# Top-k attention and GELU MLP on one core: the last 64 rows' P turned by VectorE squares and DRAM instead of by TensorE

## The chip, the cores and the metric

The kernel runs on one core of a Trainium2 chip. The metric is the device time of one launch in microseconds; three runs of the kernel before gave 1480.06 us in the median (1479.93 to 1480.07). PE is TensorE (PEld its weight loads), DVE VectorE, ACT ScalarE, POOL GpSimd, SP the engine whose queue issues most DMAs.

## The reference

Eight batches, eight heads, 576 rows, head size 64. Per head, only the 32 largest scores of a row take part in the softmax; the attention's output, as 4608 tokens of width 512, goes through an MLP with an exact GELU. All is float32.

```python
scores = scale * np.matmul(q, k.transpose(0, 1, 3, 2))
kth = np.partition(scores, -32, axis=-1)[..., -32:-31]
scores = np.where(scores >= kth, scores, -1e9)
attn = np.exp(scores - max); attn = attn / (sum + 1e-9)
x = (attn @ v) as (B*S, H*D)          # 4608 x 512
out = gelu_exact(x @ w_in) @ w_out    # 512 -> 2048 -> 512
```

## The kernel before

**Items and slots.** Two heads make a pair, four pairs (`NP`) a batch. A pair's 576 query rows are four tiles of 128 (`t` = 0 to 3, `NM` = 4) and 64 last rows (`TL`). An item is one tile of one pair: 128 rows for two heads, 2 x 576 scores in one tile `s`. The last 64 rows of two pairs share one item (`t == NM`), so a batch has 16 main items and 2 of last rows, 144 items in all (`N`). Even batches put the two items of last rows at their end, odd batches at their start (`starts` holds each batch's first item). So four items of last rows stand together four times: 16 to 19, 52 to 55, 88 to 91 and 124 to 127. Below, such a group from 52 on is called a boundary; there are three.

**The slot.** One loop (`for n in range(ahead)`) writes out the order of every engine by hand; pass n is slot n. In slot n: scores of items n+2 and n+3 (in even slots), into PSUM and from there by ACT into `s` (L394); the products with v of item n-3 (`attend`, L715 and L726); the transposes of item n-2 (`transposes`: `tails` L619/L622 and `both` L649, copied by ACT into `pt`, L664); `select` and `softmax` of item n-1 on ACT (L517, L529); `top_k` of item n on DVE (MAX8 and MATCH_REPLACE8, L483 and L486), which ends with `inverse` (L504, the reciprocal of item n-1's sums) and has `square_p` in its middle; on POOL `threshold` (L497, L498), `normalise` (L552), two passes over the scores for the lists (L447, L455), `add_small` (L510); and MLP pieces (`mlp`): `h_ps` (L773), then `gelus` on ACT (L789, with a table load), sums of the gelus on POOL (L810 to L813), `seven_piece` (L927) and the `y_ps` products (L929), whose parts POOL adds up (L950, L979 to L994).

**Two ways to turn P.** The products need P with the keys on the partitions. For most items PE transposes it: one matmul of `tails` (two for an item of last rows) and eight of `both`, and ACT copies them from PSUM. For an item that `squared(i)` names (even main items from 28 on), DVE transposes `s` in squares of 32 x 32 in place (L569), four DMAs of SP write it to a DRAM tile `turned` (L579) at the end of slot i+2, and four read it back (L586) into `pt` at the start of slot i+3. `pt` has one buffer for two items, so a read waits until the products of the items before are done; last rows use the left half of `pt` and a tile of their own, `pt_end`, item by item.

**What is shared.** From slot 13 on (`few`), one PSUM bank `z` serves the last keys' scores, the tails' transposes, the `seven` product and the attention output `o` in turn: each waits until ACT has copied the one before it out. The first of two score tiles in an even slot shares its banks with `h_ps`. `issue` holds a v load back to the end of the slot (`flush`) where a square's DMAs come first (`held`). `room_in` says how many MLP pieces a slot gets.

```python
    def squared(i):
        return SINGLE.stop - 2 < i < N - 2 and i % 2 == 0 and items[i][1] < NM and i % RINGS != 12
```

Of the kernel before, what the change touches and what calls it, by code (L numbers as in the profile page):

```python
# [8 lines left out]
TOPK = 32  # L9
# [5 lines left out]
def kernel(  # L15
# [95 lines left out]
    def load(n, pair, queue=None, queue2=None):  # L111
        if pair >= n_pairs:
            return
        queue = queue or nc.sync
        queue2 = queue2 or queue
        b, h0 = pair // NP, 2 * (pair % NP)
        src = sources[n]
        if n != "v" and pair >= SQUARES:
            t = flat[n][0]
            for e in range(2):  # L120
                for d in range(2):
# [8 lines left out]
        for e in range(2):  # L130
            queue.dma_start(
                out=t[:, 0:NM, e, :], in_=src[b, h0 + e, 0:SM].rearrange("(t p) d -> p t d", p=P)
            )
            queue2.dma_start(out=t[e * TL : (e + 1) * TL, NM, e, :], in_=src[b, h0 + e, SM:S])
# [35 lines left out]
    low = const.tile([P, 1], f32, name="low")  # L170
    nc.gpsimd.memset(low, -EXP0 * 2.0**20)
    high = const.tile([P, 1], f32, name="high")
# [103 lines left out]
    def transpose_qk(pair, first=False):  # L276
# [4 lines left out]
        def squares(c):  # L281
            rq, rk, kt = flat["q"][0], flat["k"][0], kt_of.get(pair)
            if c == 0:
                nc.vector.transpose(kt[:, 0:q_tail], rk)
            elif c == 1:
                nc.vector.transpose(kt[:, q_tail:], rq[:, SM:])
            else:
                nc.vector.transpose(q_of[pair], rq[:, 0:SM])

        def by_pe(c):  # L290
            rq, rk = raw_of("q", pair), raw_of("k", pair)
            group = (
                [(rk, j) for j in range(NM)], [(rk, NM), (rq, NM)], [(rq, j) for j in range(NM)]
            )[c]
            tp = bank("tp_qk")
            for x, (r, j) in enumerate(group):
                nc.tensor.transpose(
                    tp[:, x * P : (x + 1) * P], r[:, j].rearrange("p e d -> p (e d)"), ident
                )
            dst = (kt_of[pair][:, 0:SM], kt_of[pair][:, SM:], q_of.get(pair))[c]  # L300
            copy = nc.vector.tensor_copy if first and c < 2 else nc.scalar.copy
            copy(out=dst, in_=tp[:, 0 : len(group) * P])

        def piece(c):
            if c == 0:
                kt_of[pair] = work.tile([P, 2 * P + SM], f32, tag="kt", bufs=NP + 2, name="kt")
# [17 lines left out]

    def row(i, e):
        return S_of[i][:, e * S : (e + 1) * S]
# [10 lines left out]
    def halves(t, e, step):  # L337

        return spread(t[:, e * TL :], step + (TL if e == 0 else -TL), TL)

# [3 lines left out]
    def last_keys(i, t_ps):  # L344
# [3 lines left out]
        if t < NM:  # L348
            nc.tensor.matmul(
                t_ps[:, 0:P], lhsT=q_of[pair][:, t * P : (t + 1) * P],  # L350
                rhs=kt_of[pair][:, SM : SM + P], start=True, stop=True,
# [8 lines left out]
        for r in range(2):  # L360
            kt = kt_of[pair + r]
            for e in range(2):
                nc.tensor.matmul(
                    t_ps[half(r, e), r * TL : (r + 1) * TL],
                    lhsT=kt[:, SM + P + e * TL : SM + P + (e + 1) * TL],
                    rhs=kt[:, SM + e * TL : SM + (e + 1) * TL],
# [3 lines left out]
            s.rearrange("p (r n) -> p r n", r=2)[:, :, SM:S],  # L370
            t_ps[:, 0:P].rearrange("p (r n) -> p r n", r=2), func=AF.Copy, scale=scale,
        )

    def scores(i, second=False):
# [3 lines left out]
        S_of[i] = s = work.tile([P, 2 * S], f32, tag="s", bufs=6, name="s")  # L378
# [3 lines left out]
        if t < NM:  # L382
            q_t, kt = q_of[pair][:, t * P : (t + 1) * P], kt_of[pair]
            for e in range(2):
                rows = slice(e * D, (e + 1) * D)
                nc.tensor.matmul(  # L386
                    s_ps[:, e], lhsT=q_t[rows, :], rhs=kt[rows, 0:SM], start=True, stop=True
# [7 lines left out]
        else:  # L395

            for r in range(2):
                kt = kt_of[pair + r]
                for e in range(2):
                    rows = slice(e * D, (e + 1) * D)  # L400
                    nc.tensor.matmul(
                        s_ps[half(r, e), r, :], lhsT=kt[rows, SM + P + e * TL : SM + P + (e + 1) * TL],
                        rhs=kt[rows, 0:SM], start=True, stop=True,
                    )
            s2 = s.rearrange("p (r n) -> p r n", r=2)
            nc.scalar.activation(s2[:, :, 0:SM], s_ps, func=AF.Copy, scale=scale)
# [50 lines left out]
    def top_k(i, last, middle):  # L457
# [4 lines left out]
            "neg": work.tile([P, 2], f32, tag="neg", name="neg"),  # L462
            "bias": work.tile([P, 2], f32, tag="bias", name="bias"),
            "den": work.tile([P, 2], f32, tag="den", name="den"),
            "rden": work.tile([P, 2], f32, tag="rden", name="rden"),
        }
        top = work.tile([P, 2, TOPK - 8], f32, tag="top", bufs=1, name="top")
        into = [st["first"]] + [top[:, :, 8 * r : 8 * r + 8] for r in range(TOPK // 8 - 1)]
# [21 lines left out]
        st["kth"] = top[:, :, TOPK - 9]  # L490
# [45 lines left out]
    def normalise(i):  # L536
# [4 lines left out]
        if i < DIAGS:  # L541
            d = work.tile([P, 2, P], f32, tag="part", bufs=3, name="diag")
# [12 lines left out]
    pt_end = const.tile([P, 2, P], f32, name="pt_end")  # L555
    nc.gpsimd.memset(pt_end, 0.0)
# [24 lines left out]
    def read_p(i):  # L581

        if squared(i):
            d = turned.pop(i)
            for k in range(P // SQ):
                nc.sync.dma_start(  # L586
                    out=pt_now[0][k * SQ : (k + 1) * SQ, :, 0:P], in_=d[:, :, k, :]
                )

    def transposes(i):  # L590
# [3 lines left out]
        if squared(i):  # L594

            def keys_only(ahead):
                pt_now[0] = work.tile([P, 2 * NM + 1, 2 * P], f32, tag="pt", bufs=1, name="pt")
# [7 lines left out]
        def tails(ahead):  # L605
# [3 lines left out]
            if t % 2 == 0:  # L609
                pt_now[0] = work.tile([P, 2 * NM + 1, 2 * P], f32, tag="pt", bufs=1, name="pt")  # L610
# [7 lines left out]
            elif t < NM:  # L618
                nc.tensor.transpose(tp[:, at : at + P], s[:, SM : S + TL], ident)  # L619
            else:  # L620
                for r in range(2):
                    nc.tensor.transpose(  # L622
                        tp[0:TL, at + r * P : at + (r + 1) * P],
                        s[:, r * S + SM : (r + 1) * S], ident,
                    )
            if keys:
                keys()
            if t < NM:
                nc.scalar.copy(
                    out=pt_now[0][:, NM, t % 2 * P : (t % 2 + 1) * P], in_=tp[:, at : at + P]  # L630
                )
                return
            for e in range(2):
                c = slice(e * TL, (e + 1) * TL)
                nc.scalar.copy(
                    out=halves(pt_end[c, 0, :], e, P),
                    in_=halves(tp[0:TL, at : at + 2 * P], e, P),
                )

        x = t % 2 * P if t < NM else 0  # L640

        def turn_over(tp, e):
            first = e * (S + TL if t < NM else S)
# [46 lines left out]

    def column(tok):
# [4 lines left out]
    def attend(i):  # L696
# [8 lines left out]
        o = bank("o")  # L705
# [15 lines left out]
        else:  # L721
            for r in range(2):
                vt = raw_of("v", pair + r)
                for j in range(NJ):
                    for e in range(2):
                        nc.tensor.matmul(  # L726
                            o[e * D : (e + 1) * D, r * TL : (r + 1) * TL], lhsT=vt[:, j, e, :],
                            rhs=pt[:, r * NJ + j, half(r, e)] if j < NM else pt_end[:, r, half(r, e)],
                            start=(j == 0), stop=(j == NJ - 1),
                        )  # L730
            copies.append(lambda: nc.scalar.copy(
                out=xT[:, at : at + 2, c],
                in_=o[:, 0 : 2 * TL].rearrange("p (r n) -> p r n", r=2),
            ))
# [63 lines left out]
    def sums(u):  # L798
# [3 lines left out]
        if u == NU - 2:  # L802
            t = work.tile([P, 2 * S], f32, tag="s", bufs=6, name="sum_s")
# [57 lines left out]
    def part_tile():  # L861
        return work.tile([P, HALF], f32, tag="part", bufs=3, name="part")
# [91 lines left out]
    def trio_piece(u, names, x):  # L954
# [19 lines left out]
        if k == 1:  # L974
            p2, p5, s7 = end_of["p2"], part_tile(), y7[0]
            end_of["p5"] = p5
# [5 lines left out]
            small.append((1, lambda: pool(y1[:, B2], s7, p5, op=add)))  # L982
            small.append((1, lambda: pool(y0[:, B2], y0[:, B2], p5, op=add)))
            return
# [105 lines left out]

    def room_in(n):
# [6 lines left out]
        return sizes[x] + (1 if x % 2 == 0 else -1)  # L1098
# [55 lines left out]
    for n in range(ahead):  # L1154

        held[0] = n < N and squared(n - 2)
        read_p(n - 3)
# [20 lines left out]
        product = attend(n - 3)  # L1178
# [31 lines left out]
        if few[0]:  # L1210
            softmax(n - 1, 0)
            if n % 2:
# [66 lines left out]
        if n == 5:  # L1279
            load("q", SQUARES)  # L1280
# [39 lines left out]
```

## Time and profile before

| what | value |
|---|---|
| runs | 1480.06 us median (1479.93 to 1480.07) |
| profiled execution | 1479.73 us, span 1478.0 us |
| granted TensorE clock | 1.0 |
| PE busy | 1461.6 us, 99% of the span, 8817 records |
| DVE, POOL, ACT busy | 88%, 77%, 74% of the span |
| DMA | 112.94 MB, mean 76 GB/s |

The profiled execution lies 1.7 us above its span and 0.33 us below the median of the runs. In a row of a group, the figures after the bar are busy time, mean ns of one, and the engine's idle time just before. In a row of the timeline they are start and length in us, and in square brackets the idle time before it with what ended it. Matmuls are pipelined, so the start of the next row tells more of what one costs than its own length. A float32 matmul leaves two records in the trace, a transpose one.

### The profile page before, as it was taken

What the parts mean: (1) busy time and instruction counts of PE and PEld (TensorE: products, weight loads), DVE (VectorE), ACT (ScalarE), POOL (GpSimd) and SP (SyncE); (2) the same over time, 40 slices, a digit from 0 to 9 for tenths busy, and PEclk for the clock granted to TensorE, in tenths of its full rate; (3) what the DMA queues carried; (4) which work ended last, traced back from release to release, by engine and by line L of the source; (5) the groups of instructions that cost most, each with busy time, mean ns of one, the idle gap of its engine ahead of it and who ended that gap; (6) DMA issues with size and microseconds to landing.
All of it is one profiled execution on the core that took longest, in us unless ns stands there. A gap on an engine that the chain in (4) does not pass through costs nothing. (4 is left out here: it accounts for less than half of the span.)

```text
span 1478.0 us, 27006 instructions
## 1 busy us (share of the span) xinstructions
PE 1461.6 (99%) x8817; PEld 1147.9 (78%) x8817; DVE 1294.3 (88%) x3318; ACT 1099.9 (74%) x1942; POOL 1140.1 (77%) x1291
## 2 busy tenths in 40 slices
PE   8999999999999999999999999999999999999999
PEld 6876677877777777887777778787777777787787
DVE  8999899999999988999999987999999997998701
ACT  7999977877777687777777778777777777776620
POOL 6877567877898879877898978886788887987732
PEclk9999999999999999999999999999999999999999
DMA  7424310045435322345534331345453421233300
GB/s 198 143 86 124 84 48 1 24 88 101 95 73 93 66 58 52 65 95 108 105 83 81 69 61 47 66 93 99 97 103 73 89 55 41 61 61 72 70 15 15
DMA packets 477645, 112.94 MB, mean 76 GB/s; under 512 B 413216, under 2 KB 469056, under 8 KB 477504
## 3 DMA queue, kind: packets, MB, share of 16 engines
q1 hardware_dynamic: 476240, 110.78, 35.3%
q8 instruction: 70, 1.15, 0.3%
q14 instruction: 71, 0.58, 0.1%
q10 hardware_dynamic: 1200, 0.39, 0.1%
q0 software_dynamic: 64, 0.03, 0.0%
HBM read 73.39 MB, written 37.75 MB: 75 GB/s over the span
## 5 line engine op out<-in xcount | busy, mean ns | idle before, releaser
L773 PE MATMUL h_ps<-xT,w_in_sb 128*128 128x256 f32 (+1 forms) x2560 | 536.2, 361 | 0.1
L773 PEld LDWEIGHTS h_ps<-xT,w_in_sb 128*128 128x128 f32 x2560 | 436.5, 190 | 73.4 <-issue 25.2
L483 DVE MAX8 top<-lists 128x8 f32<-128x576 f32 (+1 forms) x792 | 476.4, 641 | 0.0
L486 DVE MATCH_REPLACE8 lists<-top,lists 128x288 f32<-128x288 f32 (+1 forms) x528 | 307.9, 589 | 0.0
L552 POOL TENSOR_TENSOR s<-s,rden 128x1152 f32<-128x1152 f32 x135 | 285.8, 2117 | 0.3 <-DVE rden L504 0.3
L529 ACT ACTIVATE s<-s,bias 128x576 f32<-128x576 f32 x288 | 225.4, 787 | 11.0 <-issue 0.4
L517 ACT ACTIVATE s<-s,neg 128x576 f32<-128x576 f32 x288 | 225.5, 793 | 1.7 <-POOL neg L497 1.6
L510 POOL TENSOR_SCALAR den<-den 128x2 f32<-128x2 f32 x144 | 31.4, 218 | 215.9 <-ACT s L529 210.2
L455 POOL TENSOR_TENSOR lists<-lists 128x576 int32<-128x576 int32 x132 | 186.2, 1410 | 4.0
L447 POOL TENSOR_TENSOR lists<-s 128x576 int32<-128x576 int32 x133 | 187.2, 1407 | 0.0
L715 PE MATMUL o<-pt,raw_v 128*64 128x256 f32 x1280 | 153.0, 384 | 1.8 <-ACT s L529 1.1
L715 PEld LDWEIGHTS o<-pt,raw_v 128*64 128x64 f32 x1280 | 87.8, 136 | 85.8 <-issue 37.2
L789 ACT ACTIVATE g<-h_ps 128x512 f32<-128x512 f32 x144 | 78.2, 594 | 100.6 <-PE h_ps L773 100.4
L929 PE MATMUL y_ps<-w_out_sb,sum 128*128 128x256 f32 x472 | 140.4, 379 | 0.0
L394 ACT ACTIVATE s<-s_ps 128x1024 f32<-128x1024 f32 x127 | 125.5, 1035 | 10.5 <-PE s_ps L386 10.3
L664 ACT COPY pt<-tp 128x1024 f32<-128x1024 f32 x85 | 86.6, 1019 | 62.2 <-PE tp L649 62.1
L386 PE MATMUL s_ps<-kt,qm 64*128 64x512 f32 x512 | 129.4, 618 | 0.8 <-ACT s L392 0.8
L504 DVE RECIPROCAL rden<-den 128x2 f32<-128x2 f32 x144 | 23.2, 161 | 108.6 <-POOL den L510 107.4
L486 DVE MATCH_REPLACE8 lists<-first,lists 128x288 f32<-128x288 f32 x264 | 114.3, 439 | 0.0
L929 PE MATMUL y_ps<-w_out_sb,g 128*128 128x256 f32 x480 | 113.4, 379 | 0.0
L483 DVE MAX8 first<-lists 128x8 f32<-128x288 f32 x268 | 106.6, 436 | 0.0
L929 PEld LDWEIGHTS y_ps<-w_out_sb,g 128*128 128x128 f32 x480 | 91.2, 190 | 12.4
(167 smaller groups left out, 2533.1 us busy)
## 6 DMA issues: line engine op xcount, KB each, us to landing
turned<-s SPq DMA_DIRECT2D x192, 144.0 KB, 3.5
pt<-turned SPq DMA_DIRECT2D x192, 144.0 KB, 3.2
raw_v<-in_v_dram SPq DMA_DIRECT2D x64, 128.0 KB, 2.4
out_dram<-y SPq DMA_DIRECT2D x30, 256.0 KB, 2.1
raw_q<-in_q_dram SPq DMA_DIRECT2D x112, 64.0 KB, 2.0
raw_k<-in_k_dram SPq DMA_DIRECT2D x112, 64.0 KB, 2.0
w_out_sb<-in_moe_w_in_dram SPq DMA_DIRECT2D x14, 511.8 KB, 4.8
w_out_sb<-in_moe_w_out_dram SPq DMA_DIRECT2D x10, 511.8 KB, 4.1
```

The lines of the kernel that those rows point to most:

```text
L386: nc.tensor.matmul(s_ps[:, e], lhsT=q_t[rows, :], rhs=kt[rows, 0:SM], start=True, stop=True)
L394: nc.scalar.activation(spread(s, S + TL, SM), s_ps, func=AF.Copy, scale=scale)
L447: nc.gpsimd.tensor_tensor(t[:, :, 1].bitcast(i32), a.bitcast(i32), b.bitcast(i32), op=ALU.add)
L455: nc.gpsimd.tensor_tensor(into_of(i)[:, :, 1].bitcast(i32), both, top, op=ALU.subtract)
L483: nc.vector.max(x[:, e], src[:, e])
L486: nc.vector.match_replace(dst[:, e], x[:, e], src[:, e], LOWEST)
L517: nc.scalar.activation(s, s, func=AF.Prelu, bias=st["neg"][:, e : e + 1], scale=1.0, alpha=STEEP)
L529: nc.scalar.activation(s, s, func=AF.Exp, bias=st["bias"][:, e : e + 1], scale=1.0, accum_out=st["den"][:, e : e + 1],)
L552: nc.gpsimd.tensor_tensor(s, s, wide, op=ALU.mult)
L715: nc.tensor.matmul(o[e * D : (e + 1) * D, 0:n], lhsT=vt[:, j, e, :], rhs=pt[:, e * NJ + j if j < NM else NM, :], start=(j == 0), stop=(j = ...
L773: nc.tensor.matmul(h_tile(u)[:, i, :], lhsT=w_in_sb[:, ko, f * P : (f + 1) * P], rhs=xT[:, ko, c0 : c0 + n], start=(ko == 0), stop=(ko == ...
L929: nc.tensor.matmul(acc[names][:, k], lhsT=lhsT, rhs=rhs, start=(j == 0 and k == 0), stop=(j == FT // 2 - 1 and k == 1),)
```

## The change

- `squared` also names every item of last rows from 27 on, even or odd: 12 items, four in each boundary. Their P goes by DVE squares, DRAM and `pt` (both halves of it); `pt_end` is gone. The four early items of last rows (16 to 19) stay with PE, with one `tails` matmul and one copy in place of two.
- The products of these items move (`delayed`): item 52 from slot 55 to the start of slot 56, 53 from the start of 56 to the middle of 57, 54 and 55 from slots 57 and 58 together into the middle of 59, where they follow `seven` on PE and share one tile in the bank `z`. The other boundaries are alike. Slot 58 gets two more MLP pieces, slot 57 two fewer.
- When a delayed item ends a batch, the next batch's v tiles are loaded with the four small DMAs of the tails on ACT's queue, in two blocks of four: at the end of slots 56 and 57.
- The score tile `s` has seven buffers, not six. The scores of last rows and the columns of `kt` are laid out as for main items, with the squares' q and k loaded by four DMAs each instead of eight.
- Small tiles: `neg`, `bias`, `den`, `rden` share a tile, `low` and `high` share one, `top` is smaller, `part` has two buffers instead of three (a part goes straight into `y1`).

```diff
     def squared(i):
-        return SINGLE.stop - 2 < i < N - 2 and i % 2 == 0 and items[i][1] < NM and i % RINGS != 12
+        if not SINGLE.stop - 2 < i < N - 2:
+            return False
+        return items[i][1] == NM or (i % 2 == 0 and i % RINGS != 12)
+
+    def delayed(i):
+        return squared(i) and items[i][1] == NM
...
-        S_of[i] = s = work.tile([P, 2 * S], f32, tag="s", bufs=6, name="s")
+        S_of[i] = s = work.tile([P, 2 * S], f32, tag="s", bufs=7, name="s")
...
-        o = bank("o")
+        both = delayed(i) and i - 1 in starts
+        o = shared.pop() if both else bank("o")
+        off = 2 * TL if both else 0
...
-                issue(lambda r=r: load("v", pair + r + NP))
+                issue(lambda r=r: load("v", pair + r + NP, None, nc.scalar if delayed(i) else None))
...
-                    for at, lo, hi, by in ((0, 0, SM, queue), (SM + e * TL, SM, S, queue2)):
-                        by.dma_start(
-                            out=t[rows, at : at + hi - lo].rearrange("i (c j) -> i c j", j=SQ),
-                            in_=src[b, h0 + e, lo:hi, cols].rearrange("(c i) j -> i c j", i=SQ),
-                        )
+                    queue.dma_start(
+                        out=t[rows, at : at + S].rearrange("i (c j) -> i c j", j=SQ),
+                        in_=src[b, h0 + e, :, cols].rearrange("(c i) j -> i c j", i=SQ),
+                    )
...
+    def bare(n):
+        return n - 4 in starts and delayed(n - 4)
...
-        return sizes[x] + (1 if x % 2 == 0 else -1)
+        return sizes[x] + (1 if x % 2 == 0 else -1) + 2 * (bare(n) - bare(n + 1))
...
         held[0] = n < N and squared(n - 2)
-        read_p(n - 3)
+        mid = [i for i in (n - 5, n - 4) if delayed(i) and n % 2 and (i % 2 or i in starts)]
+        if not mid:
+            read_p(n - 3)
...
-        product = attend(n - 3)
+        if delayed(n - 4) and n % 2 == 0 and n - 4 not in starts:
+            product = attend(n - 4)
+        else:
+            product = not delayed(n - 3) and attend(n - 3)
...
         if few[0]:
             softmax(n - 1, 0)
+            if mid:
+                for i in mid:
+                    attend(i)
+                copy_x()
+                read_p(n - 3)
             if n % 2:
                 mlp(ODD)
...
     def part_tile():
-        return work.tile([P, HALF], f32, tag="part", bufs=3, name="part")
+        return work.tile([P, HALF], f32, tag="part", bufs=2, name="part")
```

More of the change, by code (lines that the diff above doesn't have):

```diff
@@ L461, in top_k @@
             "first": work.tile([P, 2, 8], f32, tag="first", name="first"),
[L462 to L465, printed above, removed]
-        }
-        top = work.tile([P, 2, TOPK - 8], f32, tag="top", bufs=1, name="top")
-        into = [st["first"]] + [top[:, :, 8 * r : 8 * r + 8] for r in range(TOPK // 8 - 1)]
+        }
+        stat = work.tile([P, 4, 2], f32, tag="stat", name="stat")
+        st.update((n, stat[:, x]) for x, n in enumerate(("neg", "bias", "den", "rden")))
+        top = work.tile([P, 2, 16], f32, tag="top", bufs=1, name="top")
+        into = [st["first"]] + [
+            top[:, :, 8:16] if r == TOPK // 8 - 1 else top[:, :, 0:8] for r in range(1, TOPK // 8)
+        ]
         if paired(i):
@@ L541, in normalise @@
         if i < DIAGS:
[L542 removed]
+            d = work.tile([P, 2, P], f32, tag="part", bufs=2, name="diag")
             nc.gpsimd.tensor_tensor(
@@ L617, in tails @@
                     )
-            elif t < NM:
+            else:
                 nc.tensor.transpose(tp[:, at : at + P], s[:, SM : S + TL], ident)
[L620 to L625, printed above, removed]
             if keys:
                 keys()
[L628 to L640, printed above, removed]
+            nc.scalar.copy(out=pt_now[0][:, NM, x : x + P], in_=tp[:, at : at + P])
+        x = i % 2 * P
         def turn_over(tp, e):
-            first = e * (S + TL if t < NM else S)
+            first = e * (S + TL)
             for j in range(NM):
```

92 lines of the change are left out of this document (55 added, 37 removed).

## The prediction

> **What bounds the kernel now.** I read the page's busy shares first, then the busy times of the engines by stretch of time, then the timeline of each engine around slots 54 to 59.
>
> ```profile
> PE 1461.6 (99%) x8817; PEld 1147.9 (78%) x8817; DVE 1294.3 (88%) x3318; ACT 1099.9 (74%) x1942; POOL 1140.1 (77%) x1291
> ...
> 526.00:570.00 44.00, 43.98 (x350) 35.33 (x348) 32.90 (x90) 34.70 (x68) 35.96 (x44) 1.00 0.18 44
> 570.00:875.00 305.00, 304.51 (x1747) 238.53 (x1743) 289.21 (x744) 229.06 (x405) 250.79 (x281) 1.00 0.43 84
> ```
>
> The columns of the two stretches are: length, then PE, PEld, DVE, ACT and POOL busy, the granted clock, the DMA share and GB/s. The first stretch is the boundary with items 52 to 55, the second the slots up to the next boundary. PE is full in both, at a granted clock of 1.00, so what PE does not have to do comes off the end, and any new wait of PE is added to it. DVE differs: 95% busy between boundaries (289.21 of 305), 75% in the boundary (32.90 of 44). The change gives DVE work just there.
>
> **What PE is spared.** In slot 57 PE turns an item of last rows:
>
> ```profile
> 563.76 0.38 PE L622 MATMUL tp_t<-ident,s 128*64 128x128 f32 x2
> 563.98 0.60 PE L929 MATMUL y_ps<-w_sum,sum 128*128 128x256 f32 x2
> ...
> 564.84 1.04 PE L649 MATMUL tp<-ident,s 128*128 128x128 f32 x8
> 565.71 0.60 PE L929 MATMUL y_ps<-w_sum,g 128*128 128x256 f32 x2
> ```
>
> From start to next start the two tails cost 0.22 us and the eight others 0.87, together 1.09 us an item; four items make 4.36 us a boundary, three boundaries 13.1. The four early items lose one tail each, 4 x 0.11 = 0.4 us. In the built program's order of instructions 124 matmuls are indeed gone (12 x 10 + 4), so that the change does nothing is no case. The products keep their number and size and only move.
>
> **What DVE and POOL get.** The reciprocal that ends each of slots 54 to 57, and one square:
>
> ```profile
> 536.76 0.17 DVE L504 RECIPROCAL rden<-den 128x2 f32<-128x2 f32 x1 [1.97 <-POOL den L510]
> 549.07 0.17 DVE L504 RECIPROCAL rden<-den 128x2 f32<-128x2 f32 x1 [4.22 <-POOL den L510]
> 559.34 0.17 DVE L504 RECIPROCAL rden<-den 128x2 f32<-128x2 f32 x1 [2.17 <-POOL den L510]
> 569.48 0.17 DVE L504 RECIPROCAL rden<-den 128x2 f32<-128x2 f32 x1 [2.05 <-POOL den L510]
> 573.39 1.36 DVE L569 STREAM_TRANSPOSE s<-s 128x1152 f32<-128x1152 f32 x1
> ...
> 559.38 0.22 POOL L497 TENSOR_SCALAR neg<-top 128x2 f32<-128x2 f32 x1
> 567.75 1.39 POOL L455 TENSOR_TENSOR lists<-lists 128x576 int32<-128x576 int32 x1
> 569.22 0.22 POOL L510 TENSOR_SCALAR den<-den 128x2 f32<-128x2 f32 x1
> ```
>
> DVE idles 1.97 + 4.22 + 2.17 + 2.05 = 10.41 us in these four slots. Four squares take 4 x 1.36 = 5.44 of that and 5 us are left, so the squares cost nothing as long as the boundary shrinks by less. DVE's own work in a slot is 549.07 - 536.76 - 4.22 = 8.09 us, with a square 9.45: two of the slots can shrink from 10.06 and 12.31 to that, by 0.6 + 2.9 = 3.5 us. The other two cannot, because POOL works through them without a gap (from `neg` at 559.38 to the end of `den` at 569.44) and the next reciprocal waits for it. So no more than 3.5 us a boundary is to be had, 3 x 3.5 + 0.4 = 10.9 in all.
>
> **The products in the middle of a slot.** They come on PE straight after `seven`, in the same PSUM bank, so they wait until ACT has copied `seven` out, and that copy stands behind the two gelus:
>
> ```profile
> 574.86 0.78 ACT L529 ACTIVATE s<-s,bias 128x576 f32<-128x576 f32 x1
> 575.54 0.19 ACT L529 ACTIVATION_READ_ACCUMULATOR s<-s,bias 128x1 f32 x1
> 575.74 1.28 ACT L789 ACT_TABLE_LOAD   x1
> 578.20 1.08 ACT L789 ACTIVATE g<-h_ps 128x512 f32<-128x512 f32 x2 [1.18 <-PE h_ps L773]
> 579.17 0.38 ACT L948 COPY p<-seven 128x256 f32<-128x256 f32 x1
> ...
> 578.00 1.03 PE L927 MATMUL seven<-w_sum,g 128*128 128x256 f32 x4
> 578.87 1.89 PE L929 MATMUL y_ps<-w_out_sb,g 128*128 128x256 f32 x8
> 580.59 0.59 PE L929 MATMUL y_ps<-w_sum,sum 128*128 128x256 f32 x2
> ```
>
> PE is free at 578.87 and the copy ends at 579.55: today the `y_ps` products fill that time, after the change PE waits 0.68 us, in slot 57 and again in 59. That is 1.36 us a boundary. The copy of `o` into `xT` follows on ACT behind a select, a table load and an exp, and PE has six products of 0.43 before it needs the bank again; I take nothing for it, and up to 0.5 in the range.
>
> **The DMAs on ACT's queue.** Two blocks of four small v loads a boundary stand in ACT's order, the first behind the last exp of slot 56 and ahead of the gelus' table load, the second behind the last exp of slot 57 and ahead of the copy of scores to `s`. Only the very start of the trace shows issues on ACT:
>
> ```profile
> 0.73 0.44 SPq L131 DMA_DIRECT2D raw_q<-in_q_dram  x1
> 0.73 1.08 ACTq L131 DMA_DIRECT2D raw_k<-in_k_dram  x2
> 1.85 1.28 ACT L302 ACT_TABLE_LOAD   x1 [1.85 <-issue]
> ```
>
> Two take 1.08 us, 0.54 each, and the table load, which waits for no one, starts right behind them. A block of four is then 2.16 us. Before the gelus ACT has 1.18 us to spare (the idle time at 578.20), so `seven`'s copy, and PE behind it, come 2.16 - 1.18 = 0.98 us later. For the second block:
>
> ```profile
> 567.54 1.99 PE L386 MATMUL s_ps<-kt,qm 64*128 64x512 f32 x8
> 569.45 0.69 PE L726 MATMUL o<-pt,raw_v 128*64 128x64 f32 x16
> ...
> 568.31 0.18 ACT L529 ACTIVATION_READ_ACCUMULATOR s<-s,bias 128x1 f32 x1
> 568.71 1.94 ACT L394 ACTIVATE s<-s_ps 128x1024 f32<-128x1024 f32 x2 [0.21 <-PE s_ps L386]
> ...
> L394 ACT ACTIVATE s<-s_ps 128x1024 f32<-128x1024 f32 x127 | 125.5, 1035 | 10.5 <-PE s_ps L386 10.3
> ```
>
> The last exp ends 0.95 us after the scores start on PE. With 2.16 of issues and 1.03 of copy the shared banks are free after 4.14 us; PE is back at them after 1.91 of scores and, new in this place, four `y_ps` products of 1.72 (578.87 to 580.59), 3.63 in all. PE waits 0.51.
>
> So a boundary gains 4.36 - 1.36 - 0.98 - 0.51 = 1.5 us if an issue costs ACT its full 0.54, and 4.36 - 1.36 = 3.0 if it costs ACT nothing, with no other gain to be had from that edit. The row is from an idle ACT; none shows issues behind a running exp, so I take the middle, 2.25, and keep both ends. Three boundaries and the early tails: 6.75 + 0.4 = 7.2 us.
>
> **P through DRAM.** Square to product, as the even main items have it today:
>
> ```profile
> 574.82 3.40 SPq L579 DMA_DIRECT2D turned<-s  x4
> 580.89 2.55 SPq L586 DMA_DIRECT2D pt<-turned  x4
> ...
> pt<-turned SPq DMA_DIRECT2D x192, 144.0 KB, 3.2
> ...
> 585.70 1.99 PE L386 MATMUL s_ps<-kt,qm 64*128 64x512 f32 x8
> 587.62 2.38 PE L715 MATMUL o<-pt,raw_v 128*64 128x256 f32 x20
> ```
>
> From the square's start at 573.39 to the last landing, 583.44 + 3.2, there are 13.2 us, 1.0 before the product. Item 52 keeps this distance of two slots, 53 to 55 get more. The tightest is new: main item 56 can be read into `pt` only after the product of 55 in the middle of slot 59. From there 2.55 + 3.2 = 5.75 us pass to the landing; PE has about 14 `y_ps`-sized matmuls' worth of products, transposes and scores until the next `o`, 8.3 us (580.59 to 587.62 is 7.0, with the four products before it 8.7, less 0.4 for waits). No wait; if SP is late by over 2.5 us, the rest is PE's.
>
> SP issues more here, 16 writes and 16 reads a boundary, but fewer for q and k (four instead of eight a tensor) and none for v's tails. Behind SP's waits stand v's main loads and the stores, needed more than a slot later. Nothing on the path.
>
> **The rest** is nothing by the rows: `s` never waited for a free buffer (the 10.3 idle us of L394 are all PE's), so seven of them only pay for P's longer stay; the shared small tiles and two `part` buffers add no wait of another engine in the built order; 64 instead of 128 columns of q's tail spare DVE some 28 x 0.1 us where it is not on the path. Each could also cost a tenth or two, the sum under 1 us.
>
> **The sum.** 1479.73 of the profiled execution less 7.2 is 1472.5; the runs' median lies 0.33 above it, so 1473.
>
> **Rivals.**
>
> *The issues run under the exp (1471).* If ACT's queue goes on to the issues while the last exp still works, they start 0.87 us earlier (574.86 to 575.73): the first block costs PE 0.11, the second nothing, the gain is 2.9 a boundary, 9.1 in all. For it: the issues wait for nothing that the exp makes. Against it: the one row shows issue and table load strictly in turn. [...] Chance 0.26.
>
> *One slow issue in four (1479).* SP's own loads of v's tails have it:
>
> ```profile
> 552.39 1.40 SPq L134 DMA_DIRECT2D raw_v<-in_v_dram  x1
> 554.52 0.47 SPq L134 DMA_DIRECT2D raw_v<-in_v_dram  x1
> ```
>
> Three of 0.47 and one of 1.40 make a block of 2.81 us: PE waits 1.63 and 1.16, the gain is 0.2 a boundary and 1.0 in all. Chance 0.15.
>
> *Slower: ACT's issues wait for SP's (1485.5).* Both blocks fall where SP writes a square, 3.40 / 4 = 0.85 us an issue. If an ACT issue waits for the one under way, half of that on average, it costs 0.54 + 0.43 = 0.97 and a block 3.88: PE waits 2.70 and 2.23, which with 1.36 outweighs 4.36 by 1.9 a boundary, 5.4 us in all. It decides from 0.73 us an issue on. Against it: at 0.73 us SP and ACT issue side by side and neither is longer than usual. [...] Chance 0.17.
>
> **How the numbers follow.** The forecast (1473, its own range 1471 to 1475.5) has 0.42. A measurement of this kernel tells about 0.2% from no change, 3 us. Forecast and first rival are faster by more: 0.68; the second is within: 0.15; the third slower: 0.17. From 1468 (the 10.9 us that POOL and DVE allow, and the 1 us left open) to 1481 (the second rival with 2 us of late reads) about 0.8 is held; the slower case lies outside.
>
> **What would show it.** Right: in the trace after, PE idles some 0.7 us and 1.7 us before `o` at L738 behind ACT's copy of `seven`, some 0.5 before `h_ps` in slot 58, and nowhere else; four squares a boundary fill DVE's waits before L519, and a boundary is 2 to 3 us shorter. Wrong: issues on ACT longer than 0.73, a wait of PE's `o` for `pt`, or a DVE reciprocal that comes later than POOL's `den`.

## The result and the profile after

| | before | after |
|---|---|---|
| runs | 1480.07 us median (1479.93 to 1480.32, 4 runs) | 1494.69 us (1493.35 to 1495.74, 4 runs) |
| profiled execution | 1479.73 us, span 1478.0 | 1493.65 us, span 1491.8 |
| granted TensorE clock | 1.0 | 0.994 |

The ratio is 1.0098 (95% interval 1.0081 to 1.0116). The changed kernel is 14.6 us slower; the forecast was 7 us faster. The page's busy times, then the second of the two stretches of the prediction (length, PE, PEld, DVE, ACT, POOL, clock, DMA share, GB/s):

```profile
PE 1455.1 (98%) x8693; PEld 1138.3 (76%) x8693; DVE 1307.8 (88%) x3331; ACT 1082.4 (73%) x1899; POOL 1141.1 (76%) x1290
...
570.00:875.00 305.00, 299.28 (x1756) 234.88 (x1755) 282.60 (x725) 221.60 (x391) 247.06 (x277) 0.99 0.45 90
```

The 124 matmuls are gone, yet PE, which was full, now idles 5.7 us in this stretch, and the mean clock there is 0.99 where it was 1.00. The waits of PE (total us, times, longest us) name the places:

```profile
PE o L738 <- DMA pt<-turned: 13.7, 3, 4.8
...
PE o L738 <- ACT y L962: 3.0, 3, 1.0
PE seven L944 <- POOL g L829: 2.1, 3, 0.7
...
PE o L738 <- ACT p L965: 1.4, 3, 0.5
```

Each of the four comes once a boundary. The reciprocals that end slots 56 to 59 on DVE date the loss:

```profile
555.60 0.17 DVE L519 RECIPROCAL stat<-stat 128x2 f32<-128x2 f32 x1 [1.09 <-POOL stat L525]
...
565.87 0.17 DVE L519 RECIPROCAL stat<-stat 128x2 f32<-128x2 f32 x1 [0.91 <-POOL stat L525]
...
575.14 0.14 DVE L519 RECIPROCAL stat<-stat 128x2 f32<-128x2 f32 x1
...
590.32 0.17 DVE L519 RECIPROCAL stat<-stat 128x2 f32<-128x2 f32 x1 [7.05 <-POOL stat L525]
```

Before, the third and the fourth of these were:

```profile
578.75 0.14 DVE L504 RECIPROCAL rden<-den 128x2 f32<-128x2 f32 x1
...
587.00 0.17 DVE L504 RECIPROCAL rden<-den 128x2 f32<-128x2 f32 x1
```

Up to the end of slot 58 the change had gained 3.6 us, and one slot later it had lost 3.3. Slot 59 took 15.18 us instead of 8.25; its sisters 95 and 131 took 17.06 and 15.96. PE's waits in the boundary, with the two products of slot 59, and the granted clock of that slot:

```profile
555.32 1.39 PE L738 MATMUL o<-pt,raw_v 128*64 128x64 f32 x40 [1.03 <-ACT y L962]
...
572.43 1.13 PE L944 MATMUL seven<-w_sum,g 128*128 128x256 f32 x4 [0.68 <-POOL g L829]
574.02 1.39 PE L738 MATMUL o<-pt,raw_v 128*64 128x64 f32 x40 [0.46 <-ACT p L965]
579.56 2.32 PE L738 MATMUL o<-pt,raw_v 128*64 128x64 f32 x40 [4.15 <-DMA pt<-turned]
581.81 2.62 PE L946 MATMUL y_ps<-w_out_sb,g 128*128 128x256 f32 x8
```

```profile
580.00:582.50 2.50, 2.50 (x38) 2.29 (x35) 2.50 (x6) 0.37 (x1) 1.15 (x1) 0.50 0.79 123
582.50:585.00 2.50, 2.50 (x12) 2.18 (x11) 0.76 (x2) 0.00 (x0) 0.00 (x0) 0.88 0.03 4
```

The product of 54 runs, then PE waits 4.15 us for item 55's P, and when it goes on the clock is 0.50: the second product takes 2.32 us where the first took 1.39. DVE's row is the square of item 55; SP's queue shows why its P was late (start, length and number of issues):

```profile
559.52 1.36 DVE L591 STREAM_TRANSPOSE s<-s 128x1152 f32<-128x1152 f32 x1
...
556.48 6.53 SPq L134 DMA_DIRECT2D raw_v<-in_v_dram  x4
563.32 2.55 SPq L611 DMA_DIRECT2D pt<-turned  x4
566.29 3.51 SPq L601 DMA_DIRECT2D turned<-s  x4
569.84 2.95 SPq L134 DMA_DIRECT2D raw_v<-in_v_dram  x4
572.90 0.92 SPq L861 DMA_DIRECT2D out_dram<-y  x2
573.91 2.56 SPq L611 DMA_DIRECT2D pt<-turned  x4
576.59 3.65 SPq L601 DMA_DIRECT2D turned<-s  x4
```

Item 55's square was done at 560.9. Its write (566.29) stood behind the loads of v0 and v1 (until 563.0, of which 3.1 us were a wait for another v DMA) and the read of item 54; its read (573.91) stood behind the loads of v2 and v3 and two stores, and by the median landing of a write, 3.6 us, the write's landing alone would have held it until about 573. It landed at 579.5; PE wanted it at 575.4.

For one boundary I added up PE's timeline from start to next start, from the `seven` of slot 53 to that of slot 63 (517.74 to 616.20 before, 517.33 to 619.52 after; 3.7 us longer). Transposes and tails take 4.4 us less, with the last keys' scores 4.7. Against that stand 6.3 us of waits (4.15, 1.03, 0.68, 0.46) and 2.1 us by which the matmuls next to these waits take longer, most of it at the lower clock.

### The profile page after: what moved, and what is told of

Same layout as the page of the kernel before. It is cut to its first block, busy times and chain, and to the rows that moved or that the text cites. A ratio compares the mean times of both kernels' runs of the same rounds, so it can differ in the third digit from the quotient of the medians.

```text
span 1491.8 us, 26509 instructions
## 1 busy us (share of the span) xinstructions
PE 1455.1 (98%) x8693; PEld 1138.3 (76%) x8693; DVE 1307.8 (88%) x3331; ACT 1082.4 (73%) x1899; POOL 1141.1 (76%) x1290
## 5 line engine op out<-in xcount | busy, mean ns | idle before, releaser
L567 POOL TENSOR_TENSOR s<-s,stat 128x1152 f32<-128x1152 f32 x135 | 285.8, 2117 | 0.3 <-DVE stat L519 0.3
L532 ACT ACTIVATE s<-s,stat 128x576 f32<-128x576 f32 x288 | 225.0, 790 | 13.0 <-POOL stat L512 12.9
L544 ACT ACTIVATE s<-s,stat 128x576 f32<-128x576 f32 x288 | 225.0, 785 | 11.3 <-POOL lists L462 0.7
L525 POOL TENSOR_SCALAR stat<-stat 128x2 f32<-128x2 f32 x144 | 31.3, 218 | 225.3 <-ACT s L544 211.1
L727 PE MATMUL o<-pt,raw_v 128*64 128x256 f32 x1280 | 152.9, 384 | 1.9 <-ACT s L544 1.3
L727 PEld LDWEIGHTS o<-pt,raw_v 128*64 128x64 f32 x1280 | 86.8, 136 | 86.7 <-issue 43.2
L519 DVE RECIPROCAL stat<-stat 128x2 f32<-128x2 f32 x144 | 23.0, 160 | 109.3 <-POOL stat L525 108.7
L946 PE MATMUL y_ps<-w_out_sb,g 128*128 128x256 f32 x480 | 117.2, 388 | 0.0
L672 ACT COPY pt<-tp 128x1024 f32<-128x1024 f32 x73 | 74.4, 1019 | 56.4 <-PE tp L657 56.3
```

Of the source, the lines that this page charges most:

```text
L532: nc.scalar.activation(s, s, func=AF.Prelu, bias=st["neg"][:, e : e + 1], scale=1.0, alpha=STEEP)
L544: nc.scalar.activation(s, s, func=AF.Exp, bias=st["bias"][:, e : e + 1], scale=1.0, accum_out=st["den"][:, e : e + 1],)
L567: nc.gpsimd.tensor_tensor(s, s, wide, op=ALU.mult)
L727: nc.tensor.matmul(o[e * D : (e + 1) * D, 0:n], lhsT=vt[:, j, e, :], rhs=pt[:, e * NJ + j if j < NM else NM, :], start=(j == 0), stop=(j = ...
L946: nc.tensor.matmul(acc[names][:, k], lhsT=lhsT, rhs=rhs, start=(j == 0 and k == 0), stop=(j == FT // 2 - 1 and k == 1),)
```

## The experiments

Items and lines are named as in the first boundary and in each kernel's own numbering. All ran beside the kernel before; its medians were 1480.1 to 1480.9.

| kernel | us, median | ratio to before (95%) |
|---|---|---|
| changed kernel | 1494.69 | 1.0098 (1.0081 to 1.0116) |
| 1 v loads late | 1489.95 | 1.0067 (1.0052 to 1.0082) |
| 2 write first | 1486.49 | 1.0043 (1.0029 to 1.0057) |
| 3 PE kept busy | 1488.60 | 1.0056 (1.0041 to 1.0071) |
| 4 last rows by PE | 1479.03 | 0.9991 (0.9982 to 1.0000) |
| 5 v loads early | 1494.21 | 1.0093 (1.0078 to 1.0108) |
| 6 = 2 and 5 | 1482.83 | 1.0017 (1.0008 to 1.0026) |
| 7 = 6, products behind `y_ps` | 1485.40 | 1.0036 (1.0023 to 1.0049) |
| 8 = 7, tails on SP | 1487.93 | 1.0053 (1.0036 to 1.0069) |
| 9 only 55 | 1483.18 | 1.0024 (1.0013 to 1.0034) |
| 10 52 and 55 | 1475.62 | 0.9967 (0.9955 to 0.9980) |
| 11 only 52 | 1473.20 | 0.9951 (0.9939 to 0.9964) |
| 12 52 and 55, at `seven` | 1475.70 | 0.9968 (0.9957 to 0.9980) |
| 13 52 and 55, copy first | 1471.98 | 0.9944 (0.9932 to 0.9957) |
| 14 = 11, six `s` | 1473.56 | 0.9952 (0.9939 to 0.9966) |
| 15 52, 54, 55 | 1474.10 | 0.9952 (0.9939 to 0.9966) |

**1. v's main loads late.** In this kernel items 54 and 55 multiply, for the pairs of v1 to v3, the v of the batch before, since those loads come behind their products.

```diff
+            if queue2 is nc.scalar and n == "v":
+                v_late.append(put)          # v0 run behind the read of 55, v1 to v3 behind that of 56
```

> Only the place of eight v main loads a boundary on SP's queue is changed: v0 goes behind the read of item 55's P, v1 to v3 behind the read of 56's. Theory A (SP's queue puts that read late: the loads for v0 and v1 stand 6.5 us on SP ahead of the read of 54, v2 and v3 another 3.0 us ahead of the read of 55): the three waits of PE's o for pt (4.15, 4.78, 4.75 us) and the slow clock behind them go; slots 59, 95 and 131, 6.9, 8.8 and 7.7 us longer than their own DVE work in the changed kernel, shrink to some 8.3 us: 1494.7 - 23.4 = 1471. Theory B (the write of 55 behind the read of 54, and the two trips through DRAM, set the time; the loads only fill SP's waits): the read starts 1.0 us earlier at most, 3 to 5 us in all: 1490 to 1492. Theory C (the 16 DMA engines are full there, mean share 0.93 to 1.13 between 570 and 580 us, so the same bytes land no earlier): 1493 to 1495.

1489.95 us. The read of 55 was issued at 571.17, 2.7 us earlier, but the waits of PE's `o` now read:

```profile
PE o L742 <- DMA raw_v<-in_v_dram: 8.2, 2, 4.2
...
PE o L742 <- ACT s L536: 3.5, 1, 3.5
```

I had missed that items 54 and 55 open the next batch and use the very v0 to v3 that are being loaded: these loads belong ahead of the products in slot 59. (The 3.5 us are the same wait, put down to another engine; v0's loads were issued at 573.75 and `o` began at 577.11.) Theories A and C miss the time; it is near B's, but for another reason: the loads are not filler on SP, they are due in the same slot as P.

**2. The write of 55 ahead of the reads.**

```diff
             write_p(n - 2)
+            if mid and held[0]:
+                read_p(n - 3)
+                read_p(n - 2)
             flush()
...
```

> The v loads of v0 and v1 stay where they are; the write of item 55 and then the reads of 54 and 55 follow each other on SP at the end of slot 57, ahead of the loads for v2 and v3 and the stores. Theory A and B both: the read of 55 is issued at about 570 instead of 573.9 and lands at about 575.6, where PE wants it at 575.4: a wait of 0.2 us is left, 1472. Theory C (DMA engines full): 1490 or more. If SP's order isn't the cause at all: 1494.7.

1486.49 us, with a granted clock of 0.995 to 1.0 over its runs. SP's order is a cause: changing nothing else takes 8 us off, so full DMA engines (theory C, 1490 or more) are not the whole of it. But the forecast of 1472 was far off, because two other DMAs came to be the last ones:

```profile
PE o L738 <- DMA raw_v<-in_v_dram: 4.8, 7, 1.5
...
PE o L727 <- DMA pt<-turned: 4.1, 3, 1.9
```

v2 and v3, now behind the reads, are late for 55's product, and the read of main item 56 is late for the product of 57 (L727).

**3. PE kept busy in the wait.**

```diff
                 for i in mid:
+                    if both_in(i):           # i - 1 in starts: item 55
+                        keep_busy(18, ident)
                     attend(i)
```

> As the changed kernel, but with 18 matmuls of 128x128 that nobody reads (0.22 us each, 4.0 us) on PE between the products of 54 and 55, where PE waits for pt. The wait itself isn't shortened. Theory A1 (the granted clock falls to 0.50 because PE idles for over 4 us, and the products behind it run at half speed): the clock stays at 1.00, each boundary gets back the work lost at the lower clock, about 1.6, 3.4 and 2.5 us: 1487. Rival (the clock falls for another reason, such as the DMAs or power; or the loss beside the idle time has nothing to do with it): 1494 to 1495.

1488.60 us, and the clock (third figure from the right) stays at 1.00 where it was 0.50:

```profile
580.00:583.00 3.00, 2.26 (x46) 1.98 (x45) 3.00 (x7) 0.37 (x1) 1.70 (x2) 1.00 0.72 116
```

```profile
575.95 4.29 PE L1136 MATMUL warm<-ident 128*128 128x128 f32 x36
580.98 1.23 PE L738 MATMUL o<-pt,raw_v 128*64 128x64 f32 x35 [0.74 <-DMA pt<-turned]
```

PE's timeline shows P as late as ever (18 matmuls of 0.22 us, 4.0, and 0.74 of idling), but of the loss of 14.6 us 8.1 are left (between the profiled executions the difference is 3.8): the rest was the price of idling, not of waiting. Theory A1 holds.

**4. Last rows by PE, the rest of the change kept.**

```diff
-        return items[i][1] == NM or (i % 2 == 0 and i % RINGS != 12)
+        return items[i][1] < NM and i % 2 == 0 and i % RINGS != 12
```

> Last rows' P by PE again, as before, with the products in their old places and v's tails on SP; seven score tiles, the shared small tiles, two part buffers, the four-DMA loads for q and k and the single early tails stay. The prediction took all this for nothing but 0.4 us: 1479.7 (1479 to 1481). If one of them costs something (a part buffer or a shared small tile that makes an engine wait), above 1481; if the loss of the changed kernel lies here and not in the squares, 1490 or more.

1479.03 us. The loss lies in the squares of last rows and their products. The rest gains 1.5 us (interval 0 to 2.7). In this kernel all 16 items of last rows spare one tail, 16 x 0.11 = 1.8 us, which would account for it; no run takes the tails alone.

**5 and 6. v's main loads early; with the write first.**

```diff
-                issue(lambda r=r: load("v", pair + r + NP, None, nc.scalar if delayed(i) else None))
+                if delayed(i):
+                    load("v", pair + r + NP, None, nc.scalar)   # mains at once, tails by issue()
+                else:
+                    issue(lambda r=r: load("v", pair + r + NP))
...
```

> The v main loads go to SP as soon as the product before them is written out (ahead of the writes of items 54 and 55), the tails stay on ACT; write of 55 still behind the read of 54. By SP's rows: loads of v0 and v1 552.6 to 556, write of 54 to 559.5, loads of v2 and v3 to 562.5, read of 54 once that write has landed, 563 to 565.5, write of 55 to 569, landed 572.6, read of 55 to 575.2, landed 578.2, against 575.4 where PE wants it: a wait of some 2.8 us instead of 4.15, with less of the slow clock: 1487 to 1490. Rival (with the loads out of the way SP is on time, order of write and read is no matter): 1476 to 1478.

> Loads of v early and the write of 55 ahead of the reads of 54 and 55: read of 55 lands at about 575, v2 and v3 at 565, read of 56 at about 585.6 with PE wanting it at 586.3. Theory (SP's queue is the whole loss beyond what ACT's copies cost): no wait of o for pt or v; a boundary gains 4.1 (PE work removed) less 2.2 (o behind ACT's two copies of seven 1.03 + 0.46, seven behind POOL 0.68) less some 0.9 of slower first matmuls behind each wait, with the 1.4 of the other edits: 1480.5 - 1.4 - 3 x 1.0 = 1476. Rival (there are further waits that come up once these go, as in the run with the write first, where o waited for v and for 56's P): 1480 or more.

Run 5 gave 1494.21: the write of 54 took 4.3 us instead of the 3.5 reckoned with and the loads of v2 and v3 4.4 instead of 3.0, so the read of 55 was issued at 575.12, even later than in the changed kernel. Moving the loads alone gains nothing. Run 6 gave 1482.83, 12 us better than the changed kernel, but 7 above the forecast and where its rival had it: the reads of 54 and 55 are still 0.5 to 1.5 us late. In it the clock fell to 0.51 behind two short waits, 0.70 and 1.48 us (PE's timeline, then the windows):

```profile
572.67 1.13 PE L953 MATMUL seven<-w_sum,g 128*128 128x256 f32 x4 [0.70 <-POOL g L838]
575.28 2.00 PE L744 MATMUL o<-pt,raw_v 128*64 128x64 f32 x36 [1.48 <-DMA pt<-turned]
```

```profile
575.00:577.00 2.00, 1.72 (x36) 1.75 (x38) 2.00 (x7) 0.63 (x1) 1.45 (x3) 0.64 1.15 248
577.00:579.00 2.00, 1.86 (x36) 1.70 (x34) 2.00 (x9) 1.92 (x3) 2.00 (x2) 0.51 1.18 262
```

**7 and 8. Products behind four `y_ps` products; and v's tails on SP.**

```diff
+            if n % 2:
+                mlp(ODD)
             if mid:
                 for i in mid:
                     attend(i)
                 copy_x()
...
-            if n % 2:
-                mlp(ODD)
```

> As the run before it, and the products of 53 and of 54 and 55 stand behind four y_ps products instead of right behind seven, so that ACT copies seven out meanwhile. Theory (the wait for ACT's copy of seven is paid in full): 3 x (1.03 + 0.46 + 0.4 of restarts) = 5.7 us less than the run before it: 1470.5. Rival (PE is at POOL's and DVE's limit there, the wait only moves to seven behind POOL or to the next use of the shared bank): as the run before it, 1475 to 1476.

> As the run before it, but v's tails on SP next to the main loads, so that ACT issues no DMA there. If ACT's issues cost PE time (they take 0.6 us each on ACT), up to 0.5 us a boundary comes back, 1469. If SP has no room for eight more issues of 0.5 us ahead of the write of 55, its read lands at about 579.5 against 577: 2.5 us or more a boundary lost: 1478 to 1482.

1485.40 and 1487.93, each above its theory and its rival. In run 7 the waits for ACT's copies of `seven` are gone. One of 2.0 us for the bank behind ACT's copy into `xT` takes their place, and that of 57's product (L733) for P grows from 2.3 us in run 6 to 4.4:

```profile
PE o L733 <- DMA pt<-turned: 4.4, 2, 2.3
...
PE o L744 <- DMA pt<-turned: 3.3, 4, 1.8
PE seven L953 <- POOL g L838: 2.3, 3, 0.8
PE t_ps L373 <- ACT xT L754: 2.0, 3, 0.7
```

The read of 56 is held by the landing of 56's own write (SP waits 2.2 us for it, until 583.54; the product of 55 was done at 579.7), and that write was issued at 575.78, behind the reads of 54 and 55 and two stores, though 56's square was done at 571.5. In run 8 the wait of 57's product is 8.1 us in all, but in the first boundary its write of 55 (565.07 against 565.26) and its read of 56 (583.48 against 583.54) stand where run 7 has them, and the ranges of the two kernels overlap (1485.0 to 1488.6 and 1483.8 to 1489.1). So moving v's tails off ACT's queue did not help; that it costs time is not shown.

**9, 10 and 11. Only some items by squares.**

```diff
-        return items[i][1] == NM or (i % 2 == 0 and i % RINGS != 12)
+        if items[i][1] == NM:
+            return i - 1 in starts or (i % 2 == 0 and i not in starts)   # run 10: 55 and 52
+        return i % 2 == 0 and i % RINGS != 12
```

In runs 9 to 15 v's tails are on SP again.

> Of the four items of last rows only the last (55, 91, 127) goes by squares and DRAM; its product stands in the middle of slot 59 behind four y_ps products. 52 to 54 stay with PE and in their old places, v's loads too; the rest is as in the run with last rows by PE (1479.0). Theory (the loss comes from three DRAM trips in a row through one queue and one pt buffer; a single trip has 10 us of room): no wait of o for pt or v; each boundary saves eight transposes and one tail (0.87 + 0.11 = 0.98 us) less at most 0.75 for the shared bank behind ACT's copy into xT: 1479.0 - 3 x (0.25 to 0.98) = 1476 to 1478.3. Rival (any product moved behind main item 56's read makes that read and the product of 57 late by 2 us): 1482 or more.

> As the run before it, and the first item of last rows (52, 88, 124) goes by squares and DRAM too, its product together with that of 53 at the start of slot 56, in one bank and copied once. Theory (trips that don't follow each other closely are free): another 0.98 us a boundary, 1473 to 1475.5. Rival (v0 and v1, now loaded a slot later, 547 to 554 by the rows of before, against 556 where item 54's product needs them, come late): a wait of o for raw_v of up to 2 us a boundary, 1476 to 1482.

> Only the first item of last rows (52, 88, 124) goes by squares and DRAM, its product together with that of 53 at the start of slot 56; 55 is with PE again, so nothing is left in the middle of slot 59. Theory (the product of 55 in the middle of 59 costs more than it saves: with it slot 59 is 9.49 us long, with last rows by PE 8.25): 1475.6 - 3 x 1.24 = 1471.9. Rival (PE is full, the 0.98 us that 55 saves per boundary stand against the 0.93 that PE waits for the bank): 1475 to 1476, no difference.

With only 55 (run 9) no `o` waits for a DMA, and the kernel still loses 4 us against run 4. ACT's and PE's timelines show where:

```profile
579.06 0.78 ACT L532 ACTIVATE s<-s,stat 128x576 f32<-128x576 f32 x1 [2.16 <-POOL stat L512]
579.90 1.28 ACT L544 ACT_TABLE_LOAD   x1
581.19 0.78 ACT L544 ACTIVATE s<-s,stat 128x576 f32<-128x576 f32 x1
...
581.97 0.24 ACT L748 COPY xT<-o 128x128 f32<-128x128 f32 x1
```

```profile
578.14 1.39 PE L738 MATMUL o<-pt,raw_v 128*64 128x64 f32 x40
...
582.26 0.49 PE L367 MATMUL tp_t<-kt,qm 128*128 128x128 f32 x2 [1.67 <-ACT xT L748]
```

The product is done at 579.5, but its copy into `xT` stands in ACT's order behind a select that waits for POOL, a table load and an exp; the last keys' scores, which need the same bank, wait 1.67 us. That is more than the 0.98 us of transposes that 55 saves: from the `seven` of slot 53 to that of 63 PE takes 99.40 us, against 98.15 in run 4. Run 10 came out 0.1 above its theory's upper end, with 0.93 us of that wait left and none for v. With 52 only (run 11), whose product is at a slot's start, the gain is 7.5 us on the kernel before and 5.8 on run 4. PE takes 96.25 us for the same stretch, 1.9 less than in run 4: 1.0 of it are transposes and the tail, 0.35 a wait for POOL that no longer occurs, the rest matmuls that follow each other more closely. Run 11's forecast (1471.9) was 1.3 too low, its rival's too high; run 9's two expectations both missed the mechanism.

**12 and 13. 52 and 55: the place of the product, and of the copy.**

```diff
-            softmax(n - 1, 0)
             if mid:
+                mlp(ODD)
                 for i in mid:
                     attend(i)
                 copy_x()
                 read_p(n - 3)
-            if n % 2:
+            softmax(n - 1, 0)
+            if n % 2 and not mid:
                 mlp(ODD)
```

(run 13; run 12 has the product where the changed kernel has it)

> Items 52 and 55 by squares, as in the run with both, but the product of 55 stands right behind seven, where the changed kernel has it. Theory (there it waits only 0.46 us for ACT's copy of seven, and the bank is free again in time for the last keys' scores, where the other place waits 0.93): 1475.6 - 3 x 0.5 = 1474. Rival (the copy into xT keeps its place on ACT behind select, table load and exp, so the last keys' scores wait as long): 1475.5 to 1477.

> Items 52 and 55 by squares, 55's product behind four y_ps products, and ACT's copy of it into xT ahead of the select and the exp of slot 59 instead of behind them. Theory (the 0.93 us are ACT's order alone): the wait goes, 1475.6 - 3 x 1.0 = 1472.6. Rival (ACT now stands still until PE has finished the product, its select starts 1.2 us later and the exp, the sums and the next reciprocal with it): 1475 to 1479.

Behind `seven` it costs the same as in run 10, as the rival had it (1475.70: waits of 0.58 for the copy of `seven` and 0.29 for the bank). With ACT's copy ahead of select and exp the wait is gone, as the theory had it: 1471.98, the lowest of all, 8.8 us under the kernel before and 1.2 under run 11. ACT stands still for the product (idle time 2.56 us), and PE waits for ACT no more than it did in run 10 (0.27 us before `h_ps`):

```profile
578.54 0.27 ACT L750 COPY xT<-o 128x128 f32<-128x128 f32 x1 [2.56 <-PE o L740]
...
579.39 0.38 PE L367 MATMUL tp_t<-kt,qm 128*128 128x128 f32 x2
```

**14. Run 11 with six tiles of scores.**

```diff
-        S_of[i] = s = work.tile([P, 2 * S], f32, tag="s", bufs=7, name="s")
+        S_of[i] = s = work.tile([P, 2 * S], f32, tag="s", bufs=6, name="s")
```

> Only item 52 by squares, with six tiles of scores instead of seven. If the seventh tile only pays for a P that stays longer in s until it is written: as the run with only 52, within 1 us. If scores wait for a free s: over 1 us a boundary more.

1473.56 us, no difference from run 11: with one item of last rows a boundary by squares the seventh tile shows no gain.

**15. 52, 54 and 55, with SP's order straightened** (v's loads at once and tails on SP, the write of 55 ahead of the reads, 54 and 55 together behind `y_ps`, ACT's copy first).

```diff
+            return i in starts or i % 2 == 0 or i - 1 in starts
...
             write_p(n - 2)
+            if n - 3 in turned and n - 3 in starts and delayed(n - 3):
+                read_p(n - 3)
+                read_p(n - 2)
```

> Items 52, 54 and 55 by squares and DRAM; the write of 55 ahead of the reads of 54 and 55, v's loads right behind the products of 52 and 53, 54 and 55 multiplied together behind four y_ps products of slot 59, ACT's copy ahead of select and exp. Theory (SP's queue alone decides; by the rows of the run with 52 and 55: v loads 546.4 to 556, write of 54 to 559.4, write of 55 561 to 564.5, reads of 54 and 55 to 570.5, landed 573.5, against 576.4 where PE wants them; read of 56 from 579, landed 584.7, against about 586): no wait, another 0.98 us a boundary less than the run with 52 and 55 and the copy first: 1469 to 1470. Rival (the read of 56 can't start before both products are done, and each lane wait of SP adds to it, as in the runs with all four): o of 57 waits 1.5 to 3 us a boundary, 1473 to 1478.

1474.10 us: no `o` of last rows waits, but the rival has the time, with a smaller wait than it named, 0.9 us a boundary, and by another mechanism (PE's waits, then SP's between 575 and 586 us):

```profile
PE o L729 <- DMA pt<-turned: 2.7, 3, 1.4
PE seven L949 <- POOL g L834: 2.4, 3, 0.8
...
SPq L613 <- DMA turned<-s: 4.0, 1, 4.0
```

The products of 54 and 55 were done at 577.7, but the read of 56 was issued at 580.73, once 56's own write had landed, and that write (572.21) had stood behind the reads of 54 and 55 and two stores. So the third item saves its transposes and gives them back as a wait of 57's product for the read of 56, and of `seven` for POOL: 2.1 us slower than run 13, from which it also differs in the place of v's loads.

## Why the prediction was wrong

**PE's spared work: right.** 4.36 us a boundary was forecast, 4.4 measured for transposes and tails. The 0.4 us of the early tails was not measured by itself: run 4's 1.5 also holds the late items' tails, 12 x 0.11 = 1.3, which belong to the 4.36.

**DVE's room: right.** The four squares lie in its waits, and DVE is 3.2 us earlier between the ends of slots 53 and 58, within the 3.5 forecast as the cap. That was no gain yet: the end of slot 59 waits for PE.

**The products behind `seven`: half right.** Waits of 1.03 in slot 57 and 0.46 in 59 stand against 0.68 + 0.98 and 0.68 forecast. Not foreseen: 0.68 us of `seven` behind POOL, which PE now outruns, and the copy into `xT`, taken for nothing, which costs 0.93 to 1.67 us in runs 9 and 10, where PE is otherwise on time.

**ACT's issues: mis-sized, the first rival had the mechanism.** Slot 56's last exp starts at 550.12, the first issue at 550.13:

```profile
550.12 0.78 ACT L544 ACTIVATE s<-s,stat 128x576 f32<-128x576 f32 x1
550.13 1.17 ACTq L138 DMA_DIRECT2D raw_v<-in_v_dram  x2
...
551.34 1.25 ACTq L138 DMA_DIRECT2D raw_v<-in_v_dram  x2
552.63 1.28 ACT L806 ACT_TABLE_LOAD   x1 [1.63 <-issue]
```

The issues run under the exp, and the table load stands behind them. An issue takes 0.61 us (median of 24), under the 0.73 from which the slower rival decides, and in slot 58 PE waits for none.

**P through DRAM: the step that failed.** "No wait; if SP is late by over 2.5 us, the rest is PE's" was worked out for main item 56, whose product did not wait in the changed kernel, and items 53 to 55 were waved through with "get more" distance. Each trip was costed alone; on SP four trips follow each other, 16 writes and 16 reads, and each stands in line behind the one before (55's write was issued 5.4 us after its square was done); a read also waits for its write's landing (116.4 us in 79 waits of the changed kernel). "Nothing on the path" was wrong: v's main loads stand ahead of the write and of the read of 55, and they are themselves due in slot 59, those of v2 and v3 2.6 us after their last issue (572.8 against 575.4). The wait that was named as a sign of failure, `o` for `pt`, is what came: 13.7 us. The order of write and reads alone is worth 8 us of the loss (run 2), with v's loads earlier 12 (run 6), and without these trips the loss is gone (run 4).

**Not in the sum at all:** what PE's idling costs beyond itself. The clock was 0.50 behind each of the three waits for P, and that is worth 4 to 6 us over three boundaries (run 3: 3.8 us between the profiled executions, 6.1 between the medians).

The slower rival had the sign, by a mechanism that did not occur: ACT's issues took 0.61 us, not 0.97.

What stays open: why v0's and v1's loads waited 3.1 us for another v DMA, and why SP's writes take up to 5.3 us there (run 7) against 3.4 before, was not isolated. A second `pt` buffer was not tried; in runs 6, 7 and 15 the read of 56 in the first boundary waited last for its own write's landing, not for `pt`.

## What to carry to other kernels

Lay out the DMA queue as a timeline of its own: each item's issue, landing and next read, in order, for all items that share it, and look up for every transfer that is moved past which consumer it has, across the edge of a batch too. In an engine's own order of instructions, try a copy that frees a shared bank ahead of whatever waits for another engine (here on ACT, 1475.6 to 1472.0 us). Where PE is full, reckon with a saved matmul the new waits that come up behind it: here 52 alone gained 7.5 us, 52 and 55 together 5 or 9 according to the place of ACT's copy, three items 7, while 55 alone lost 3 and all four lost 15 (each with the 1.5 us of the rest of the change).

## What the runs showed of the hardware

After some of its waits PE paid twice. Behind 4.15 us of idling the granted clock was 0.50 from 580.0 to 582.5 us and 0.88 in the 2.5 us after, and behind 4.78 us near 930 it was 0.57, 0.50, 0.50 and 0.73 in the four windows of 2 us from 931 to 939; with PE kept busy through the same wait (run 3) it stayed at 1.00. It fell behind shorter waits as well: in run 6 behind 0.70 and 1.48 us with 1.1 us of matmuls between them (0.51), and in run 7 behind one of 1.78 us (0.50), while one of 2.29 us in the same run left it at 1.00 (from 586 to 590 us). The rows are of run 7:

```profile
1278.43 1.39 PE L744 MATMUL o<-pt,raw_v 128*64 128x64 f32 x40 [1.78 <-DMA pt<-turned]
...
1280.00:1282.00 2.00, 2.00 (x7) 1.63 (x7) 2.00 (x6) 0.22 (x1) 1.23 (x1) 0.50 0.83 130
...
588.76 2.38 PE L733 MATMUL o<-pt,raw_v 128*64 128x256 f32 x20 [2.29 <-DMA pt<-turned]
```

So in these runs a wait of 1.78 us was followed by half the clock and one of 2.29 us was not: the length of one wait does not decide it, and what else does is not shown.
